# Attention order: the weight conversion's sum on VectorE with two more stops, q and k loaded one block sooner, x joined one block later

## The chip, the cores and the metric

The kernel runs on one core of one Trainium2 chip. The metric is the device time of one execution in microseconds (us). Before the change three runs took 835.17, 841.61 and 843.53 us; their median is 841.61 us.

Names used below: PE is TensorE, DVE is VectorE, ACT is ScalarE, POOL is GpSimd, SP is the engine whose one queue issues all DMAs of this kernel.

## What is computed

Clustered attention over 2 batches, 8 heads, 768 positions and head size 64, and then two gated feed-forward layers on its output. Cut to what matters:

```python
q_assign = np.argmax(np.einsum('bhsd,hcd->bhsc', q_n, c_n), axis=-1)   # nearest of 16 centroids
k_assign = np.argmax(np.einsum('bhsd,hcd->bhsc', k_n, c_n), axis=-1)
scores = np.where(q_assign[..., None] == k_assign[:, :, None, :], scale * q @ k.T, -1e9)
attn = softmax(scores); x = (attn @ v)                      # 1536 tokens x 512
x = ((x @ w1) * (x @ w2)) @ w3 @ w_out                      # d_ff = 1024
out = (sigmoid(x @ w_gate) * (x @ w_val)) @ w_out2          # d_ff = 1536
```

The weights arrive as 64-bit floats, two 32-bit words an element. The kernel turns each into a float32 pair (a rounded high part and the rest) and multiplies in three products (`mm3`).

## The kernel before

**Attention.** The 16 heads go as 8 pairs (`pr` 0 to 7). A pair has 6 blocks of 256 query rows (`at` 0 to 5); the loop at line 493 runs over all 48 blocks, `i`. For each block PE makes scores (128x768 tiles `s`), DVE their maxima (`nm`, line 348), ACT the exponentials (`e`, line 359), PE transposes these (`pt`, line 369), ACT copies the transposed tile to its high part (`ph`, line 387) and DVE makes the rest (`pl`, line 398); in three blocks of six one of the three pieces goes by way of a copy `pc` to POOL, which makes both parts. PE then multiplies by v (`av`, lines 410 and 411), and ACT copies the result to `xa` (line 419).

**Order by hand.** Inside `tc.manual_schedule` every engine, and SP's queue, executes in exactly the order in which the loop body is written. An instruction that waits holds up all that stands behind it on its engine. The work of other pairs is sprinkled over the six blocks:

- `load_qk(later)` asks for q and k (`raw`) of the pair after next, in block 1; `prep_split(later)` takes them on ACT in blocks 3 and 4 (`hi`, lines 236 and 56); `prep_scatter` copies the parts to their places with 6 DMAs per head.
- `take_x` also joins the two heads of the previous pair, in block 1: two DMAs into `xb` and a third, into `xa`, that has to wait for the first. `add_x` (POOL, block 3) adds the halves and fetches the row sums `r`; `norm_x` and `split_x` (POOL, block 5) finish that pair's 768 tokens of `x`.

**Conversion.** `f64_steps` turns one 128x512 half of a weight into its pair of parts: DMA, magnitude on ACT (line 108), clamp, shift, or, and, product (lines 115 to 124, all DVE here), sum (line 125, `f_engine`), high part on ACT (line 126), rest on POOL (line 127). It is a generator, and `convert(1)` runs it to its next `yield`: once in each of the blocks 2, 3, 4 and 5 of pairs 1 to 7, which makes 28 calls. Four halves are converted in this way: `w12_0_0`, `w12_0_1`, `w12_1_0`, `w12_1_1` (rows call their tiles `w_f`, `w_a` and `w`). The last piece of a half, from the product to the rest, runs in one go, and in the same call as the next half's DMA, so a half takes 6 calls. `convert(99)` behind the loop runs what is left.

**After attention** the scheduler, not the hand, sets the order. `g_unit(m, u)` multiplies x of 512 tokens by `wt[m]`; units (0,0) and (1,0) need tokens of batch 0 only, (0,1) needs the last pair. The other halves (`w_out` as `wo`, `w12`, `w3T`) are converted by the same generator, with a tile `w_t` in PSUM (lines 110 to 127), in 3 rotating buffers; the scheduler lets their first DMAs, ACT and POOL passes run already during attention, when a buffer is free. `w34_unit(0)` is the first to need `w3T`.

Of the kernel before, what the change touches and what calls it, by code (L numbers as in the profile page):

```python
# [8 lines left out]
F32 = mybir.dt.float32  # L9
# [6 lines left out]
B, H, S, D, C = 2, 8, 768, 64, 16  # L16
# [11 lines left out]
def tile_cluster_attention__then__moe__then__gated_moe(  # L28
# [15 lines left out]
    nc = tc.nc  # L44
# [16 lines left out]
    def move(dst, src):  # L61
        nc.sync.dma_start(dst.bitcast(F32), src.bitcast(F32))  # L62
# [36 lines left out]
    def f64_steps(src, hi, lo, name, f_engine, lo_engine):  # L99
# [22 lines left out]
        nc.vector.tensor_scalar(out=t, in0=high, scalar1=0xFF800000, scalar2=None, op0=ALU.bitwise_and)  # L122
        yield
        nc.vector.scalar_tensor_tensor(out=tf, in0=low, scalar=2.0 ** -52, in1=tf, op0=ALU.mult, op1=ALU.mult)
        f_engine.tensor_tensor(out=af, in0=high.bitcast(F32), in1=tf, op=ALU.add)
        nc.scalar.copy(hi, af)  # L126
        lo_engine.tensor_tensor(out=lo, in0=af, in1=hi, op=ALU.subtract)  # L127

    def pair_steps(src, m, what, f_engine):
        hl = ws.tile([128, 2, 2, NP, 128], F32R, tag="hl", name=f"{what}{m}")  # L130
        return hl, [
            f64_steps(src[m, w], hl[:, 0, w].rearrange("p k c -> p (k c)"), hl[:, 1, w].rearrange("p k c -> p (k c)"),
                      f"{what}{m}_{w}", f_engine, nc.gpsimd)
            for w in range(2)
        ]
# [277 lines left out]
    def take_x(i):  # L413
        if i not in avs:
            return
        pr, e, q0 = blocks[i]
        if q0 == 0:
            acc_x[pr, e] = core.tile([128, S], F32, tag=f"xa{e}", name=f"xa{pr}_{e}", bufs=2 - e)
        nc.scalar.copy(acc_x[pr, e][:, q0 : q0 + 256], avs.pop(i))  # L419
        if (e, q0) == (1, 512):  # L420

            xa, x1 = acc_x[pr, 0], acc_x.pop((pr, 1))
            xb = core.tile([128, S], F32, tag="xb", name=f"xb{pr}", bufs=1)
            move(xb[0:64], xa[64:128])
            move(xb[64:128], x1[0:64])
            move(xa[64:128], x1[64:128])
            acc_x[pr, "xb"] = xb

    def sums(pr):

# [53 lines left out]
                steps.pop(0)  # L484

    for m in range(2):
        hl, st = pair_steps(w12, m, "w12_", nc.gpsimd)
        wt.append(hl)
        steps += st
    with tc.manual_schedule(engines={mybir.EngineType.PE, mybir.EngineType.DVE, mybir.EngineType.Activation, mybir.EngineType.Pool, mybir.EngineType.SP}):  # L490
        for e in range(2):
            prep_v(0, e)
        for i in range(-2, NB + 2):
# [11 lines left out]
                prep_code(nxt)  # L505
            if nxt and at == 1:
                prep_scatter(nxt, 1)
            if later and at == 1:
                load_qk(later)
            split_lo(i - 1, 2)  # L510
            split_hi(i, 0)
            split_lo(i, 0)
# [60 lines left out]
            if 0 < pr < NPR and at == 3:  # L573
                convert(1)
        convert(99)
        for stage in (add_x, norm_x, split_x):
            stage(NPR - 1)
    att.close()

# [183 lines left out]
```

## Time and profile before

| what | value |
|---|---|
| three runs | 835.17, 841.61, 843.53 us |
| profiled execution, time | 838.32 us |
| its span, first to last instruction | 836.5 us |
| PE busy | 783.5 us, 94% |
| DVE, ACT, POOL busy | 581.8, 346.1, 348.1 us |
| pairs 1 to 5 of attention | 33.7 to 39.0 us each |
| pair 6 | 27.2 us |

A pair's stretch runs here from the reciprocal of the row sums of the pair before to its own. Busy time of an engine says how long instructions were in flight on it; a row of a timeline gives the start, the duration and in brackets how long the engine stood idle before it, and what ended that.

### The profile page before, as it was taken

How to read it: one execution, taken by the hardware profiler on the slowest of the kernel's cores; microseconds unless marked ns; L12 is line 12 of the kernel's file. 1: busy time of each engine (PE TensorE's matmuls, PEld its weight loads, DVE VectorE, ACT ScalarE, POOL GpSimd, SP SyncE). 2: the span in 40 equal slices, each digit the busy share in tenths (PEclk: the TensorE clock that was granted, in tenths of full speed). 3: DMA queues.
4: the chain of work that ended last, by engine and by line, in shares of the span. 5: the costliest groups of instructions: out<-in, count | busy, mean ns of one | idle time of the engine just before them, and what ended most of it. 6: DMA issues, size and time to landing. Idle time of an engine off the chain costs nothing.

```text
span 836.5 us, 11135 instructions
## 1 busy us (share of the span) xinstructions
PE 783.5 (94%) x4053; PEld 668.7 (80%) x4053; DVE 581.8 (70%) x848; ACT 346.1 (41%) x662; POOL 348.1 (42%) x358
## 2 busy tenths in 40 slices
PE   6897969879699889999999999999999999999998
PEld 5787958778598768887888888888888888888886
DVE  3797979879789757998899653177762577737322
ACT  1787767677578713443334221232232232013100
POOL 3354775557666634554445211034340343214200
PEclk8998999999889999999999999999999999999999
DMA  7558475484843142443444110012230122200012
GB/s 210 120 128 215 113 195 125 113 212 103 209 131 83 54 123 76 151 146 121 138 139 138 51 51 0 1 51 76 94 107 27 50 76 77 75 26 1 1 55 96
DMA packets 28887, 82.77 MB, mean 99 GB/s; under 512 B 4800, under 2 KB 4896, under 8 KB 28832
## 3 DMA queue, kind: packets, MB, share of 16 engines
q1 hardware_dynamic: 28832, 82.05, 34.2%
q8 instruction: 32, 0.52, 0.2%
q14 instruction: 23, 0.19, 0.1%
HBM read 52.49 MB, written 3.19 MB: 67 GB/s over the span
## 4 chain that ended last, share of the span: by engine, by line
PE 65%; DVE 9%; POOL 7%; DMA 7%; issue 6%; ACT 4%; SPq 2%; DVEq 0%; POOLq 0%; ACTq 0%
PE p L66 16%; PE p L67 16%; PE p L65 16%; PE pt L369 2%; PE av L410 2%; DMA w_f<-in_w_dram 2%; DVE nm L348 2%; DMA r<-r_dram 2%; PE av L411 2%; SPq L62 1%; DMA w_f<-in_w3T_dram 1%; PE w34p L67 1%; DVE pl L398 1%; PE w34p L66 1%; PE w34p L65 1%
## 5 line engine op out<-in xcount | busy, mean ns | idle before, releaser
L410 PE MATMUL av<-ph,vx 128*128 128x256 f32 x288 | 84.4, 320 | 35.3 <-ACT xa L419 34.7
L65 PE MATMUL p<-x,wgv 128*128 128x512 f32 x288 | 112.0, 389 | 0.0
L66 PE MATMUL p<-x,wgv 128*128 128x512 f32 x288 | 112.0, 389 | 0.0
L67 PE MATMUL p<-x,wgv 128*128 128x512 f32 x288 | 112.0, 389 | 0.0
L398 DVE TENSOR_TENSOR pl<-pt,ph 128x512 fp32r<-128x512 f32 x120 | 80.0, 682 | 32.0 <-ACT ph L387 30.6
L348 DVE TENSOR_REDUCE nm<-s 128x1 f32<-128x768 f32 x96 | 90.5, 944 | 11.0 <-PE s L341 10.5
L359 ACT ACTIVATE e<-s,nm 128x768 f32<-128x768 f32 x96 | 87.3, 909 | 20.0 <-DVE nm L348 18.9
L410 PEld LDWEIGHTS av<-ph,vx 128*128 128x128 f32 x288 | 57.0, 198 | 43.1 <-POOL w L127 16.1
L369 PE MATMUL pt<-ident,e 128*128 128x128 f32 x576 | 81.8, 280 | 0.6 <-DVE pl L398 0.6
L387 ACT CAST ph<-pt 128x512 fp32r<-128x512 f32 x120 | 69.1, 593 | 25.3 <-PE pt L369 23.8
L66 PE MATMUL p<-x,w 128*128 128x512 f32 x192 | 75.4, 393 | 1.4 <-POOL x L59 1.4
L411 PE MATMUL av<-pl,vx 128*128 128x256 f32 x288 | 76.1, 291 | 0.5 <-DVE pl L398 0.5
L65 PE MATMUL p<-x,w 128*128 128x512 f32 x192 | 75.5, 393 | 1.0 <-POOL x L54 1.0
L67 PE MATMUL p<-x,w 128*128 128x512 f32 x192 | 75.4, 393 | 0.0
L369 PEld LDWEIGHTS pt<-ident,e 128*128 128x128 f32 x576 | 70.0, 146 | 5.4 <-PE pt L369 0.9
L54 POOL TENSOR_SCALAR u<-ut 128x512 fp32r<-128x512 f32 x36 | 22.3, 620 | 112.1 <-DVE ut L689 112.1
L67 PEld LDWEIGHTS p<-x,wgv 128*128 128x128 f32 x288 | 54.1, 188 | 11.3
L65 PEld LDWEIGHTS p<-x,wgv 128*128 128x128 f32 x288 | 54.1, 188 | 11.2
L66 PEld LDWEIGHTS p<-x,wgv 128*128 128x128 f32 x288 | 54.1, 188 | 11.1
L127 POOL TENSOR_TENSOR wo<-wo_a,wo 128x512 fp32r<-128x512 f32 x20 | 26.3, 1313 | 81.0 <-ACT wo L126 81.0
L59 DVE TENSOR_TENSOR u<-ut,u 128x512 fp32r<-128x512 f32 x36 | 35.7, 991 | 34.1 <-POOL u L54 32.9
L411 PEld LDWEIGHTS av<-pl,vx 128*128 128x128 f32 x288 | 57.6, 200 | 0.7 <-DVE pl L398 0.7
(142 smaller groups left out, 1852.2 us busy)
## 6 DMA issues: line engine op xcount, KB each, us to landing
wgv_f<-in_w_gv_dram SPq DMA_DIRECT2D x24, 512.0 KB, 3.3
wo_f<-in_w_out_dram SPq DMA_DIRECT2D x20, 512.0 KB, 3.1
w_f<-in_w_dram SPq DMA_DIRECT2D x16, 512.0 KB, 3.2
w_f<-in_w3T_dram SPq DMA_DIRECT2D x16, 512.0 KB, 3.3
raw<-in_qkT_dram SPq DMA_DIRECT2D x16, 384.0 KB, 3.3
vraw<-in_v_dram SPq DMA_DIRECT2D x8, 384.0 KB, 4.1
QH<-hi SPq DMA_DIRECT2D x16, 192.0 KB, 5.7
KH<-hi SPq DMA_DIRECT2D x16, 192.0 KB, 3.6
```

Source lines behind the costliest of these rows:

```text
L59: lo_engine.tensor_tensor(out=lo, in0=x, in1=hi, op=ALU.subtract)
L65: nc.tensor.matmul(ps, whi, xhi, start=start, stop=False)
L66: nc.tensor.matmul(ps, whi, xlo, start=False, stop=False)
L67: nc.tensor.matmul(ps, wlo, xhi, start=False, stop=stop)
L127: lo_engine.tensor_tensor(out=lo, in0=af, in1=hi, op=ALU.subtract)
L348: nc.vector.tensor_reduce(out=nms[j], in_=sps[j][:, 0:S], axis=AX.X, op=ALU.max, negate=True)
L359: nc.scalar.activation(et, sps.pop(j)[:, 0:S], AF.Exp, bias=nms.pop(j), accum_out=acc_x[pr, "sum"][:, at : at + 1])
L369: nc.tensor.transpose(pt[:, kk, 128 * t : 128 * t + 128], exps[2 * i + t][:, k0 : k0 + 128], ident)
L387: nc.scalar.copy(ph, pt)
L398: nc.vector.tensor_tensor(out=pl, in0=src, in1=ph, op=ALU.subtract)
L410: nc.tensor.matmul(avs[i], w, ph[:, kk, :], start=kt == 0, stop=False)
L411: nc.tensor.matmul(avs[i], w, pl[:, kk, :], start=False, stop=kt == KT - 1)
```

## The change

Four edits. The sum of the four hand-scheduled halves goes from POOL to DVE. Two `yield`s are added, one before and one behind the sum, so a half takes 8 calls and not 6; with 28 calls three halves and the first four calls of the fourth stay inside the loop, and the rest of `w12_1_1` is run by `convert(99)`. `load_qk` moves from block 1 to block 0. The join of x becomes a function of its own, called in block 2.

```diff
         nc.vector.scalar_tensor_tensor(out=tf, in0=low, scalar=2.0 ** -52, in1=tf, op0=ALU.mult, op1=ALU.mult)
+        yield
         f_engine.tensor_tensor(out=af, in0=high.bitcast(F32), in1=tf, op=ALU.add)
+        yield
         nc.scalar.copy(hi, af)
         lo_engine.tensor_tensor(out=lo, in0=af, in1=hi, op=ALU.subtract)
...
         nc.scalar.copy(acc_x[pr, e][:, q0 : q0 + 256], avs.pop(i))
-        if (e, q0) == (1, 512):
-
-            xa, x1 = acc_x[pr, 0], acc_x.pop((pr, 1))
-            xb = core.tile([128, S], F32, tag="xb", name=f"xb{pr}", bufs=1)
-            move(xb[0:64], xa[64:128])
-            move(xb[64:128], x1[0:64])
-            move(xa[64:128], x1[64:128])
-            acc_x[pr, "xb"] = xb
+
+    def join_x(pr):
+
+        xa, x1 = acc_x[pr, 0], acc_x.pop((pr, 1))
+        xb = core.tile([128, S], F32, tag="xb", name=f"xb{pr}", bufs=1)
+        move(xb[0:64], xa[64:128])
+        move(xb[64:128], x1[0:64])
+        move(xa[64:128], x1[64:128])
+        acc_x[pr, "xb"] = xb
...
     for m in range(2):
-        hl, st = pair_steps(w12, m, "w12_", nc.gpsimd)
+        hl, st = pair_steps(w12, m, "w12_", nc.vector)
...
-            if later and at == 1:
+            if later and at == 0:
                 load_qk(later)
+            if at == 2 and 0 < pr and i < NB:
+                join_x(pr - 1)
...
         convert(99)
-        for stage in (add_x, norm_x, split_x):
+        for stage in (join_x, add_x, norm_x, split_x):
             stage(NPR - 1)
```

Three places show how the instructions move. In the changed program the lines behind the edits are 2 or 3 higher (125 is 126, 127 is 129, 439 is 442, 448 is 451).

**POOL, pair 2, blocks 4 and 5.** `ph` and `pl` are the parts of a transposed tile, `lo` the rest of k for pair 4, `w_0_0_a` the half under conversion, `xa` with `r` the norm of pair 1. Before:

```order
L54 TENSOR_SCALAR ph_0_1534<-pc_1536 128x512
L59 TENSOR_TENSOR pl_0_1535<-pc_1536,ph_0_1534 128x512
L59 TENSOR_TENSOR lo_1_1544<-raw_1_1327,hi_1_1543 128x768
L125 TENSOR_TENSOR w_0_0_a<-w_0_0_f_962,w_0_0_a 128x512
L127 TENSOR_TENSOR w_0_291<-w_0_0_a,w_0_291 128x512
L448 TENSOR_TENSOR xa_0_929<-xa_0_929,r_1472 128x768
```

After, the same place:

```order
L54 TENSOR_SCALAR ph_0_1534<-pc_1536 128x512
L59 TENSOR_TENSOR pl_0_1535<-pc_1536,ph_0_1534 128x512
L59 TENSOR_TENSOR lo_1_1544<-raw_1_1243,hi_1_1543 128x768
L451 TENSOR_TENSOR xa_0_925<-xa_0_925,r_1472 128x768
L54 TENSOR_SCALAR x<-xa_0_925 128x768
```

The sum is gone from POOL, and the rest (`w_0_291`) stands a pair's half later, in block 2 of pair 3; ACT's high part of the same half moved with it.

**SP's queue, from the row sums of pair 0 on, that is pair 1.** `QH`, `KH`, `QX` and `KX` are `prep_scatter`'s, `vraw` is v, `raw` q and k of pair 3. Before:

```order
L436 DMA r_dram<-rt_757 12x128
L216 DMA vraw_814<-in_v_dram 128x768
L62 DMA xb_847<-xa_0_485 64x768
L62 DMA xb_847<-xa_1_690 64x768
L62 DMA xa_0_485<-xa_1_690 64x768
L62 DMA QH_1_862<-hi_0_579 64x768
L62 DMA KH_1_863<-hi_1_644 64x768
L62 DMA QX_1_864<-hi_0_579 64x768
L62 DMA QX_1_864<-lo_0_580 64x768
L62 DMA KX_1_865<-lo_1_645 64x768
L62 DMA KX_1_865<-hi_1_644 64x768
L211 DMA raw_0_872<-in_qkT_dram 128x768
```

After:

```order
L439 DMA r_dram<-rt_757 12x128
L213 DMA raw_0_788<-in_qkT_dram 128x768
L213 DMA raw_1_790<-in_qkT_dram 128x768
L218 DMA vraw_818<-in_v_dram 128x768
L62 DMA QH_1_862<-hi_0_579 64x768
L62 DMA KH_1_863<-hi_1_644 64x768
L62 DMA QX_1_864<-hi_0_579 64x768
L62 DMA QX_1_864<-lo_0_580 64x768
L62 DMA KX_1_865<-lo_1_645 64x768
L62 DMA KX_1_865<-hi_1_644 64x768
L62 DMA xb_937<-xa_0_485 64x768
L62 DMA xb_937<-xa_1_690 64x768
```

The two loads of q and k moved past v, the join and the six scatters, to the head; the join moved behind the scatters.

**POOL, the end of attention.** `xa_0_3597` (before) and `xa_0_3583` (after) is the last pair's x, `xa_0_3200` and `xa_0_3186` that of pair 6, `wo` the first half of `w_out`. Before:

```order
L448 TENSOR_TENSOR xa_0_3200<-xa_0_3200,r_3680 128x768
L54 TENSOR_SCALAR x<-xa_0_3200 128x768
L59 TENSOR_TENSOR x<-xa_0_3200,x 128x768
L439 TENSOR_TENSOR xa_0_3597<-xa_0_3597,xb_3843 128x768
L448 TENSOR_TENSOR xa_0_3597<-xa_0_3597,r_3848 128x768
L54 TENSOR_SCALAR x<-xa_0_3597 128x768
L59 TENSOR_TENSOR x<-xa_0_3597,x 128x768
L127 TENSOR_TENSOR wo<-wo_a,wo 128x512
```

After:

```order
L451 TENSOR_TENSOR xa_0_3186<-xa_0_3186,r_3671 128x768
L54 TENSOR_SCALAR x<-xa_0_3186 128x768
L110 TENSOR_SCALAR wo_a<-wo_a 128x512
L59 TENSOR_TENSOR x<-xa_0_3186,x 128x768
L110 TENSOR_SCALAR w_2_0_a<-w_2_0_a 128x512
L129 TENSOR_TENSOR w_1_292<-w_1_1_a,w_1_292 128x512
L442 TENSOR_TENSOR xa_0_3583<-xa_0_3583,xb_3843 128x768
L110 TENSOR_SCALAR w_2_1_a<-w_2_1_a 128x512
L451 TENSOR_TENSOR xa_0_3583<-xa_0_3583,r_3848 128x768
L54 TENSOR_SCALAR x<-xa_0_3583 128x768
L59 TENSOR_TENSOR x<-xa_0_3583,x 128x768
```

The rest of `w12_1_1` (`w_1_292`) now stands ahead of the last pair's addition, and the clamp of `w_2_1` between that addition and the norm; the clamps of `wo` and `w_2_0` came here from pair 6.

## Rows read from the trace of the kernel before

**Rows 1.** The page: the span, and part 1, busy time of each engine.

```profile
span 836.5 us, 11135 instructions
...
PE 783.5 (94%) x4053; PEld 668.7 (80%) x4053; DVE 581.8 (70%) x848; ACT 346.1 (41%) x662; POOL 348.1 (42%) x358
```

**Rows 2.** Busy time by stretch, the pairs 1, 2, 4, 5 and 6 of attention; columns: stretch and its length, PE, PE's weight loads, DVE, ACT and POOL busy (instructions), granted clock as a share of full speed, DMA share, GB/s.

```profile
58.40:92.50 34.10, 29.36 (x204) 27.11 (x203) 28.34 (x39) 24.46 (x51) 20.45 (x18) 0.90 0.66 161
92.50:129.20 36.70, 29.03 (x203) 26.66 (x202) 29.58 (x41) 24.98 (x53) 23.56 (x20) 0.95 0.60 150
...
162.90:198.40 35.50, 29.22 (x204) 26.81 (x204) 30.07 (x40) 24.87 (x52) 23.35 (x20) 0.95 0.61 155
198.40:237.40 39.00, 31.49 (x202) 29.05 (x201) 29.68 (x40) 25.05 (x53) 23.53 (x20) 0.87 0.58 141
237.40:264.60 27.20, 26.73 (x198) 24.54 (x198) 26.16 (x38) 22.64 (x49) 19.84 (x20) 1.00 0.56 148
```

**Rows 3.** Who waited for whom, from 25 to 293 us; us in total, times, longest.

```profile
PE av L410 <- ACT xa L419: 34.7, 18, 5.1
...
ACT w L126 <- POOL w_a L125: 15.7, 4, 4.5
```

**Rows 4.** Timeline of PE: the eight starts of `av` behind an idle time that the prediction counts.

```profile
81.42 0.58 PE L410 MATMUL av<-ph,vx 128*128 128x256 f32 x1 [4.74 <-ACT xa L419]
...
113.30 0.38 PE L410 MATMUL av<-ph,vx 128*128 128x256 f32 x1 [1.18 <-ACT xa L419]
122.77 0.42 PE L410 MATMUL av<-ph,vx 128*128 128x256 f32 x1 [5.06 <-ACT xa L419]
...
150.12 0.38 PE L410 MATMUL av<-ph,vx 128*128 128x256 f32 x1 [1.59 <-ACT xa L419]
...
181.06 0.55 PE L410 MATMUL av<-ph,vx 128*128 128x256 f32 x1 [4.18 <-ACT xa L419]
...
220.67 0.39 PE L410 MATMUL av<-ph,vx 128*128 128x256 f32 x1 [2.65 <-ACT xa L419]
230.15 0.55 PE L410 MATMUL av<-ph,vx 128*128 128x256 f32 x1 [3.47 <-ACT xa L419]
...
281.03 0.36 PE L410 MATMUL av<-ph,vx 128*128 128x256 f32 x1 [2.52 <-ACT xa L419]
```

**Rows 5.** Timeline of ACT: `hi` of q in pairs 1, 2, 3 and 5, one magnitude (line 108) and one high part of the conversion (line 126).

```profile
77.03 0.84 ACT L236 ACTIVATE hi<-raw 128x768 fp32r<-128x768 f32 x1 [2.56 <-DMA raw<-in_qkT_dram]
80.44 0.66 ACT L108 ACTIVATE w_a<-w_f 128x512 f32<-128x512 f32 x1 [1.21 <-DMA w_f<-in_w_dram]
...
110.77 0.85 ACT L236 ACTIVATE hi<-raw 128x768 fp32r<-128x768 f32 x1 [1.10 <-issue]
...
120.37 0.62 ACT L126 CAST w<-w_a 128x512 fp32r<-128x512 f32 x1 [4.53 <-POOL w_a L125]
...
147.59 0.85 ACT L236 ACTIVATE hi<-raw 128x768 fp32r<-128x768 f32 x1 [1.55 <-issue]
...
218.15 0.84 ACT L236 ACTIVATE hi<-raw 128x768 fp32r<-128x768 f32 x1 [2.62 <-DMA QH<-ohT]
```

**Rows 6.** Timeline of POOL in pair 2, in front of ACT's high part at 120.37.

```profile
116.84 2.25 POOL L59 TENSOR_TENSOR lo<-raw,hi 128x768 fp32r<-128x768 f32 x1
119.05 1.28 POOL L125 TENSOR_TENSOR w_a<-w_f,w_a 128x512 f32<-128x512 f32 x1
121.06 1.27 POOL L127 TENSOR_TENSOR w<-w_a,w 128x512 fp32r<-128x512 f32 x1 [0.73 <-ACT w L126]
```

**Rows 7.** Timeline of SP's queue in pair 2 (a duration is that of the issue).

```profile
92.61 0.33 SPq L436 DMA_DIRECT2D r_dram<-rt  x1
96.11 0.36 SPq L216 DMA_DIRECT2D vraw<-in_v_dram  x1
...
106.66 1.20 SPq L211 DMA_DIRECT2D raw<-in_qkT_dram  x2
```

**Rows 8.** The lines of the conversion, the forms that run during attention; ns shortest, median, longest, first and last start.

```profile
L115 DVE TENSOR_SCALAR w_a<-w_a x4: 415/1414/1516, 83.8 to 248.8; 128x512 f32<-128x512 f32 x4
...
L118 DVE TENSOR_SCALAR w_a<-w_a x4: 414/536/779, 89.3 to 255.4; 128x512 uint32<-128x512 uint32 x4
...
L120 DVE SCALAR_TENSOR_TENSOR w_f<-w_f,w_a x4: 1090/1600/1780, 103.8 to 257.3; 128x512 uint32<-128x512 uint32 x4
...
L122 DVE TENSOR_SCALAR w_a<-w_f x4: 416/416/771, 112.7 to 262.3; 128x512 uint32<-128x512 uint32 x4
...
L124 DVE SCALAR_TENSOR_TENSOR w_a<-w_f,w_a x4: 921/1680/1777, 115.7 to 275.3; 128x512 f32<-128x512 uint32 x4
```

**Rows 9.** Timelines of PE and POOL at the end of attention: PE's wait for the last `pl`, POOL's last addition of x, PE's two waits for the last pair's x.

```profile
293.15 0.38 PE L411 MATMUL av<-pl,vx 128*128 128x256 f32 x1 [0.45 <-DVE pl L398]
...
298.30 1.85 POOL L439 TENSOR_TENSOR xa<-xa,xb 128x768 f32<-128x768 f32 x1 [5.43 <-DMA xa<-xa]
...
307.73 0.49 PE L65 MATMUL p<-x,w 128*128 128x512 f32 x1 [1.02 <-POOL x L54]
309.62 0.50 PE L66 MATMUL p<-x,w 128*128 128x512 f32 x1 [1.39 <-POOL x L59]
```

**Rows 10.** Who waited for whom, PE alone, from 300 us to the end: one of three lines.

```profile
PE w34p L67 <- POOL w L127: 0.6, 1, 0.6
```

**Rows 11.** Busy time by stretch, 300 to 320 us (columns as in rows 2).

```profile
300.00:320.00 20.00, 17.59 (x69) 13.84 (x68) 8.39 (x13) 3.37 (x7) 7.77 (x7) 0.91 0.37 123
```

## The prediction, made before the changed kernel ran

> **What bounds the kernel now.** Read the page first: PE is busy 94% of an 836.5 us span [rows 1], so what can be won is the time in which PE stands still. The list of waits puts nearly all of that in one place: in attention PE's `av` waits 34.7 us, 18 times, put down to ACT's copy `xa` [rows 3]. A copy of 0.4 us is not slow; it stands behind something on ACT. The stretches by pair then show what a pair costs with and without these waits: pair 6 takes 27.2 us with PE busy for 26.73, while pairs 1, 2, 4 and 5 take 34.1 to 39.0 with about the same PE work [rows 2]. They also show the second engine in line: DVE is busy for 26.16 of the 27.2 us of pair 6, and for about 28 to 30 us in the others [rows 2]. So a pair can't shrink below what DVE needs, some 28 to 31 us.
>
> The timelines say what holds ACT up. Two causes cover eight of PE's waits. (a) The conversion's high part (line 126) waits for the sum on POOL: 15.7 us on ACT in four times [rows 3]. The sum takes only 1.28 us, but it stands in POOL's queue behind the 2.25 us of `lo`, and ACT stops for 4.53 us [rows 5, 6], with the exponentials and `xa` behind it. PE's four waits from it are 5.06, 4.18, 3.47 and 2.52, together 15.2 us [rows 4]. (b) `hi` of q waits for the load: 2.56, 1.10, 1.55 and 2.62 us on ACT, and a magnitude 1.21 more behind the first [rows 5]. PE's waits from these are 4.74, 1.18, 1.59 and 2.65, together 10.2 us [rows 4]. The list names other releasers for two of the four ("issue"); the load is the last one issued ahead of them, so I count them with it.
>
> **The change, part by part.**
>
> *The two stops and the sum on DVE.* ACT's high part now runs in a later call than the sum; between them lie blocks of other work, so ACT finds the sum done. Wait (a) goes: -15.2 us. In its place DVE gets three sums in attention (the fourth comes behind the loop). No row of before has a DVE sum with both operands and result in SBUF. The nearest is the product of line 124, same shape, one operand strided: 0.921 to 1.777 us, median 1.68 [rows 8]; below nothing is excluded, since the engine has to read 512 elements. I take 1.68. The calls also move between pairs: even pairs now carry or, and, product and sum, odd pairs only clamp and shift. By the medians of rows 8 a full even pair is 1.60 + 0.42 + 1.68 + 1.68 = 5.4 us. Pair 2 had the first three, so +1.7. Pair 4 had product, clamp and shift, 3.6, so +1.7. Pair 6 had clamp, shift, or and and, 4.0, so +1.4. Pairs 3 and 5 get lighter by about 2 us each, which I count at nothing since PE bounds them. DVE is the engine next in line in even pairs, so I let all 4.8 us come back to PE. The bounds: nothing, if DVE fills the gaps in which it waits now, and 7 us, with every instruction at its longest.
>
> The Trainium skill has a rule that speaks against this edit: SBUF — State Buffer, "Who interferes with whom", says that a VectorE instruction with two SBUF inputs and a GpSimd instruction that reads SBUF exclude each other for the whole instruction. The trace agrees in kind: the product takes 0.921 us at its shortest and 1.777 at its longest [rows 8]. By the rule the three sums would cost their longest, 5.3 us, by the row's median 5.0; what it would do to POOL is a rival below.
>
> *q and k sooner.* What matters is SP's queue, not the block: the load stands at 106.66 us behind v, the join and six scatters, though the queue passed `r_dram` at 92.61 [rows 7]. The new place is right behind `r_dram`, ahead of v, which waits until 96.11 for its buffer. The loads' own buffers are free by then (`lo` of k was read in block 4). So they go out some 13 us sooner, against waits of 1.1 to 2.6 us on ACT [rows 5]. Wait (b) goes: -10.2 us. If the load went out only a block sooner (about 5 us) it would still do. The magnitude's DMA behind it also gets out sooner, since the two loads are no longer in front.
>
> *x later.* The scatters move ahead of the join by three DMAs, the join behind six; SP sends it about 5 us later, and POOL's addition is two blocks away, about 9 us at 27.2 / 6 = 4.5 us a block [rows 2]. Cost: none, by a thin margin. What hides it is POOL's own slack, busy 23.56 of 36.7 us [rows 2]; without that cover it would cost 1 or 2 us in each of seven pairs.
>
> *The handover.* `w12_1_1` is now half done when attention ends. The last `pl` ends at about 293.1 (PE starts on it at 293.15 [rows 9]). Behind it DVE has or, and, one shift of `wo`, the product, an or of `wo`, the sum. With the shortest of rows 8 that is 1.09 + 0.42 + 0.41 + 0.92 + 1.09 + 0.92 = 4.9 us, with the medians 1.60 + 0.42 + 0.54 + 1.68 + 1.60 + 1.68 = 7.5. Then 0.62 on ACT and 1.27 on POOL [rows 5, 6]: done at 299.9 to 302.5. POOL's last addition stands behind that and started at 298.30 [rows 9]: it is late by 1.6 to 4.2 us. I take 2.8, about the middle, since POOL, whose instructions stretch DVE's, is nearly idle here. PE, which waited 1.02 and 1.39 us for the x that comes of it [rows 9], waits that much longer: +2.8. `wt[1]` itself is in time, since PE asks for its second half only after the 36 products of unit (0,0) and the first half of (1,0), at 17.59 / 69 = 0.25 us each [rows 11] near 302.5. Conversions later on are just in time (PE waits 0.6 us once for the rest of a `w3T` half [rows 10]). I let them slip with PE and cost that at nothing, because DVE is busy for only 8.39 us of the 20 behind 300 [rows 11]; without that cover it is up to 4 us.
>
> **Sum.** -15.2 - 10.2 + 4.8 + 2.8 = -17.8 us. From the profiled execution, 836.5 + 1.8 around the span = 838.3, that gives 820.5. The median of the three runs is 841.6, 3.3 above the profiled execution, the lowest 835.2, below it. I add half of the 3.3 and forecast 822 us.
>
> **The rivals.**
>
> 1. *More than the sum.* After its long waits PE runs slowly for a while: pair 5 has a granted clock of 0.87 and 31.49 us of PE busy, pair 6 1.00 and 26.73 [rows 2]. Without the waits that comes back too, and pairs 3 and 5 lose DVE work. Pairs 1 to 5 at pair 6's 27.2 and 1.4 for the centroid products that it lacks would be 28.6, pairs 2 and 4 with 1.7 more. Against lengths of 34.1, 36.7, 33.7, 35.5 and 39.0 that is 32.6 off; with pair 6 1.4 longer, pair 7 2.5 shorter and the handover 2.8, -31 at the utmost. Half way from the sum: 815.
>
> 2. *DVE and POOL take over.* If each of three sums collides with a POOL instruction in front of it or behind, DVE and POOL both lose up to 1.7 us a time, and the exponentials, which wait for DVE's maxima, stop PE in ACT's place; half of the 25.4 us stays. -12.7 + 4.8 + 2.8 = -5.1, with the same additions 835. For it: DVE is 96% busy in pair 6 [rows 2]. Against: while ACT stops DVE idles too, so the room for the sums is there. By that rule of the skill's page this is where the time would end; the trace agrees as to the long products, and can't show the sums.
>
> 3. *The load doesn't go sooner*, because SP is held up ahead of it. Then only (a) goes: -15.2 + 4.8 + 2.8 = -7.6, 832. Against: the queue stands at `r_dram` 14 us before the load [rows 7].
>
> 4. *Slower: the handover grows.* The late half moves the last addition, the norm behind the clamp of `w_2_1`, and every conversion behind them; since these are just in time, PE would wait again at `w34_unit(0)`. It decides when the lateness passes 20.6 us, of which my bounds (4.2 and 4) explain 8.2. At 29 it would be 848.
>
> **Chances.** The sum as it stands, 815 to 829: 0.66. Rival 1: 0.10. Rival 2: 0.14. Rival 3: 0.06. Rival 4: 0.04. The range 812 to 832 leaves out rival 4, most of rival 2 and the end of rival 1, together under 2 in 10. A measurement of this kernel tells 1% from no change, that is below 833.2 and above 850. Faster holds the first case, rival 1, rival 3 and a third of rival 2: 0.86; the same 0.11; slower 0.03.
>
> **What would show it.** In the profile after: no wait of ACT's conversion copy for a sum; SP's load right behind `r_dram` and no wait of `hi`; `av`'s waits for `xa` near 35 - 25 + 5 = 14 us, in pairs 2, 4 and 6 and behind DVE's maxima; pairs 3 and 5 under 31 us; sums on DVE of 0.9 to 1.8 us; PE's wait for the last x near 5 us. The forecast is wrong if the waits come back under another name (maxima, `pl`), if POOL waits for the join in block 3, or if PE's wait behind 300 us passes 10 us.

## The result and the profile after

The changed kernel takes 817.86 us in the median of 4 runs (814.42 to 818.6), the kernel before 840.31 in the median of 4 (the three above and one of 839.01): a ratio of 0.973 with a 95% interval of 0.967 to 0.979. The forecast was 822 in a range of 812 to 832, so the time lies inside it. The profiled execution went from a span of 836.5 us to 816.5.

The page of the kernel after, the rows that answer to [rows 1]:

```profile
span 816.5 us, 11135 instructions
...
PE 776.9 (95%) x4053; PEld 662.3 (81%) x4053; DVE 584.3 (72%) x852; ACT 346.1 (42%) x662; POOL 344.2 (42%) x354
```

Where did the 20 us go? The best way in is to cut both executions at the same two events, the reciprocals that end pair 0 and pair 7. Busy time by stretch of the kernel before (stretch and length, PE, PE's weight loads, DVE, ACT, POOL, granted clock, DMA share, GB/s):

```profile
0.00:57.55 57.55, 46.48 (x306) 41.80 (x307) 39.18 (x61) 32.75 (x63) 22.37 (x35) 0.94 0.67 165
57.55:291.61 234.06, 199.31 (x1387) 183.37 (x1386) 194.46 (x262) 167.54 (x353) 147.00 (x130) 0.94 0.55 139
291.61:836.50 544.89, 537.69 (x2364) 443.57 (x2363) 348.19 (x526) 145.76 (x248) 178.71 (x194) 1.00 0.22 75
```

The same three stretches after:

```profile
0.00:59.96 59.96, 49.52 (x306) 44.88 (x307) 39.27 (x62) 32.86 (x63) 22.53 (x35) 0.89 0.64 158
59.96:271.22 211.26, 191.09 (x1387) 175.10 (x1386) 194.16 (x261) 166.23 (x351) 139.28 (x122) 0.99 0.58 152
271.22:816.50 545.28, 536.27 (x2364) 442.29 (x2363) 350.87 (x530) 147.04 (x250) 182.37 (x198) 1.00 0.23 76
```

Read the middle rows. Pairs 1 to 7 became 22.8 us shorter. PE's idle time there (length less busy) fell from 34.75 to 20.17, by 14.6; its busy time fell by 8.2 for the same 1387 matmuls, at a granted clock of 0.99 where it was 0.94. Pair 0 became 2.4 longer, at a lower clock; the rest of the program, the handover included, 0.4 longer. -22.8 + 2.4 + 0.4 = -20.0, the difference of the spans.

By pair, the pairs 1 to 6 after (columns as before; these answer to [rows 2]). One row there is cut at other events than the rest: its pair 6 begins at the end of one reciprocal and ends at the start of the next, 1.1 us short. Cut as below, pair 6 of the kernel before takes 28.28 us and not 27.20:

```profile
236.34:264.62 28.28, 27.80 (x205) 25.53 (x204) 27.11 (x39) 23.09 (x50) 19.86 (x20) 1.00 0.54 143
```

After:

```profile
59.96:91.28 31.32, 27.57 (x203) 25.37 (x202) 28.36 (x39) 24.20 (x50) 20.40 (x18) 1.00 0.68 177
91.28:122.47 31.19, 27.81 (x205) 25.52 (x204) 30.25 (x40) 23.80 (x51) 21.39 (x19) 1.00 0.63 159
122.47:153.26 30.79, 27.60 (x201) 25.12 (x200) 28.23 (x38) 24.67 (x53) 21.67 (x20) 1.00 0.68 178
153.26:184.44 31.18, 27.82 (x205) 25.52 (x204) 30.24 (x40) 23.81 (x51) 21.37 (x19) 1.00 0.63 159
184.44:216.88 32.44, 28.64 (x200) 26.33 (x199) 28.52 (x39) 25.31 (x56) 21.66 (x20) 0.95 0.66 169
216.88:246.04 29.16, 27.78 (x205) 25.56 (x204) 28.27 (x39) 22.09 (x46) 19.09 (x18) 1.00 0.41 103
```

Pairs 1 to 5 are now alike, 30.8 to 32.4 us. In the even ones DVE is busy for all but one us of the length: there it leaves no room, as the extra sum below shows. In the odd ones it is busy for 28.2 to 28.5, and PE still stands still for over 3 us. The waits of the kernel after, from 25 to 275 us (us in total, times, longest), say at what:

```profile
ACT e L361 <- DVE nm L350: 27.6, 39, 2.0
PE av L412 <- ACT xa L421: 20.5, 20, 2.0
```

No wait of ACT for the sum is left in this stretch, and none of `hi` for the load. PE's starts of `av` behind an idle time, against [rows 4]:

```profile
81.07 0.39 PE L412 MATMUL av<-ph,vx 128*128 128x256 f32 x1 [2.01 <-ACT xa L421]
...
87.24 0.35 PE L412 MATMUL av<-ph,vx 128*128 128x256 f32 x1 [1.74 <-ACT xa L421]
...
107.39 0.36 PE L412 MATMUL av<-ph,vx 128*128 128x256 f32 x1 [1.35 <-ACT xa L421]
...
118.16 0.36 PE L412 MATMUL av<-ph,vx 128*128 128x256 f32 x1 [2.01 <-ACT xa L421]
...
149.22 0.35 PE L412 MATMUL av<-ph,vx 128*128 128x256 f32 x1 [1.74 <-ACT xa L421]
```

None is longer than 2.01, and eleven are of 1.00 us or more. Eight of the eleven stand behind DVE. For the one at 149.22, in pair 3, DVE's timeline and ACT's:

```profile
144.13 1.35 DVE L240 SCALAR_TENSOR_TENSOR lo<-raw,hi 128x768 fp32r<-128x768 f32 x1
145.41 1.51 DVE L115 TENSOR_SCALAR w_a<-w_a 128x512 f32<-128x512 f32 x1
146.84 0.94 DVE L350 TENSOR_REDUCE nm<-s 128x1 f32<-128x768 f32 x1
...
147.82 0.90 ACT L361 ACTIVATE e<-s,nm 128x768 f32<-128x768 f32 x1 [1.73 <-DVE nm L350]
```

The maximum `nm` stands behind the rest of q and the conversion's clamp, together 2.8 us; the exponential waits 1.73 for it, `xa` stands behind the exponential, and PE waits 1.74. Pairs 1 and 5 have the same wait. In even pairs the clamp's place is taken by the product (waits of 2.01 and 1.99), and another maximum stands behind `or` (three waits of 1.35).

The other three, 2.01, 1.00 and 1.57 us, one in each odd pair, stand behind the conversion's magnitude on ACT. In pairs 1 and 5 that waits for its DMA, 1.16 and 0.64 us; in pair 3 it has no wait, and ACT is busy all the while with `hi`, an exponential and the magnitude. The one in pair 1, ahead of the wait at 81.07:

```profile
80.10 0.66 ACT L108 ACTIVATE w_a<-w_f 128x512 f32<-128x512 f32 x1 [1.16 <-DMA w_f<-in_w_dram]
80.66 0.36 ACT L421 COPY xa<-av 128x256 f32<-128x256 f32 x1
```

SP's queue in pair 2, against [rows 7]: the load of q and k now goes out right behind `r_dram`, 14 us sooner, and v no later than before.

```profile
92.25 0.33 SPq L439 DMA_DIRECT2D r_dram<-rt  x1
92.63 0.82 SPq L213 DMA_DIRECT2D raw<-in_qkT_dram  x2
95.76 0.33 SPq L218 DMA_DIRECT2D vraw<-in_v_dram  x1
```

### The profile page after: what moved, and what is told of

The parts are those of the page before. It is cut to its first block, busy times and chain, and to the rows that moved or that the text cites. A ratio compares the mean times of both kernels' runs of the same rounds, so it can differ in the third digit from the quotient of the medians.

```text
span 816.5 us, 11135 instructions
## 1 busy us (share of the span) xinstructions
PE 776.9 (95%) x4053; PEld 662.3 (81%) x4053; DVE 584.3 (72%) x852; ACT 346.1 (42%) x662; POOL 344.2 (42%) x354
## 3 DMA queue, kind: packets, MB, share of 16 engines
q1 hardware_dynamic: 28832, 82.05, 34.7%
## 4 chain that ended last, share of the span: by engine, by line
PE 65%; DVE 12%; DMA 6%; POOL 5%; issue 5%; ACT 4%; SPq 2%; DVEq 0%; ACTq 0%; POOLq 0%
PE p L66 17%; PE p L67 17%; PE p L65 17%; PE pt L371 3%; DVE nm L350 2%; DVE pl L400 2%; PE av L412 2%; DMA w_f<-in_w3T_dram 2%; PE sims L270 1%; PE av L413 1%; PE w34p L67 1%; PE w34p L66 1%; PE w34p L65 1%; DMA xb<-xa 1%; SPq L62 1%
## 5 line engine op out<-in xcount | busy, mean ns | idle before, releaser
L412 PE MATMUL av<-ph,vx 128*128 128x256 f32 x288 | 80.9, 310 | 20.8 <-ACT xa L421 20.5
L361 ACT ACTIVATE e<-s,nm 128x768 f32<-128x768 f32 x96 | 87.3, 909 | 28.6 <-DVE nm L350 27.6
L400 DVE TENSOR_TENSOR pl<-pt,ph 128x512 fp32r<-128x512 f32 x120 | 79.8, 680 | 14.2 <-ACT ph L389 11.9
L412 PEld LDWEIGHTS av<-ph,vx 128*128 128x128 f32 x288 | 54.5, 189 | 28.7 <-POOL lo L59 10.3
L413 PE MATMUL av<-pl,vx 128*128 128x256 f32 x288 | 72.8, 282 | 0.5 <-DVE pl L400 0.5
L54 POOL TENSOR_SCALAR u<-ut 128x512 fp32r<-128x512 f32 x36 | 22.3, 619 | 112.1 <-DVE ut L694 112.1
L59 DVE TENSOR_TENSOR u<-ut,u 128x512 fp32r<-128x512 f32 x36 | 35.7, 991 | 34.1 <-POOL u L54 32.9
L694 DVE TENSOR_TENSOR ut<-p,ut 128x512 f32<-128x512 f32 x36 | 24.7, 686 | 44.4 <-PE p L67 44.3
```

The lines of the kernel that those rows point to most:

```text
L59: lo_engine.tensor_tensor(out=lo, in0=x, in1=hi, op=ALU.subtract)
L361: nc.scalar.activation(et, sps.pop(j)[:, 0:S], AF.Exp, bias=nms.pop(j), accum_out=acc_x[pr, "sum"][:, at : at + 1])
L400: nc.vector.tensor_tensor(out=pl, in0=src, in1=ph, op=ALU.subtract)
L412: nc.tensor.matmul(avs[i], w, ph[:, kk, :], start=kt == 0, stop=False)
L413: nc.tensor.matmul(avs[i], w, pl[:, kk, :], start=False, stop=kt == KT - 1)
```

## The experiments

Each kernel was timed on one chip with the kernel before in the same batch (medians of before: 838.7, 837.99 and 838.04 us in three batches). All ratios are to before.

### Which edit brings the time: each alone, and both without the join

*The two stops and the sum on DVE, alone* (from the kernel before):

```diff
+        yield
         f_engine.tensor_tensor(out=af, in0=high.bitcast(F32), in1=tf, op=ALU.add)
+        yield
...
-        hl, st = pair_steps(w12, m, "w12_", nc.gpsimd)
+        hl, st = pair_steps(w12, m, "w12_", nc.vector)
```

> The kernel before with the two stops and the sum on VectorE alone; load and join stay where they were. If the prediction's sum is right, ACT's conversion copy no longer waits for a sum (15.7 us gone), PE's four waits behind it (15.2 us) go, up to 4.8 us come back through VectorE and about 2 at the handover: span 826 to 830 us, and ACT still waits for the load of q in four pairs (about 8 us). If the two causes overlap, so that removing one exposes the other, the span stays above 832 us and the waits for the load grow by as much.

Measured: 831.76 us, ratio 0.994 (0.989 to 1.000): by the interval no gain is shown for this edit alone. The profiled span, 829.5 us, is in the first branch, but what happened is the second: ACT's waits for the sum are gone and waits for DMAs have grown (below).

*The load of q and k in block 0, alone* (from the kernel before):

```diff
-            if later and at == 1:
+            if later and at == 0:
                 load_qk(later)
```

> The kernel before with q and k asked for one block sooner alone. If the prediction's sum is right, ACT's waits for the load go and with them PE's 10.2 us: span about 826 us, ACT's four waits for the sum on POOL (15.7 us) stay. If the join, which in this kernel still stands ahead of the six scatters, was what held the load up, the load goes out sooner all the same but the scatters behind it run late, and the gain is under 5 us: span above 831 us.

Measured: 832.86 us, ratio 0.994 (0.991 to 0.997): 5.8 us by the medians, where 10.2 were expected. The profiled span, 833.7 us, is in the second branch. The waits for the load in pairs 2, 3 and 5 are gone. But in pair 1 the magnitude now waits 2.39 us for its DMA and PE still 3.24, where it was 4.74; and in pair 5, where PE no longer waits for the load, its wait for the sum on POOL grew from 3.47 to 5.04, while ACT's stayed (4.54 and 4.52).

*Both, with the join of x back in block 1* (from the kernel after):

```diff
             take_x(i - 2)
+            if at == 1 and 0 < pr and i < NB:
+                join_x(pr - 1)
...
-            if at == 2 and 0 < pr and i < NB:
-                join_x(pr - 1)
```

> The changed kernel with the join of x put back into block 1, ahead of the scatters. The prediction costs the later join at nothing: span within 1.5 us of the changed kernel's 816.5. If moving the join was part of the gain (it keeps SP from stopping for its first DMA ahead of the scatters), the span is 3 us or more above it; if the later join costs something at POOL's addition, where the profile of the changed kernel shows waits of 0.4 to 1.0 us, it is 1 to 3 us below.

Measured: 819.9 us, ratio 0.979 (0.975 to 0.982).

The two edits are not two sums that add. By the medians each alone is worth 0.6%, both together 2.1%. Pairs 1 to 7 of each profiled execution, worked out from the stretches by pair as above:

| kernel | length, us | PE busy | PE idle |
|---|---|---|---|
| before | 234.06 | 199.31 | 34.75 |
| stops and sum on DVE | 227.27 | 195.50 | 31.77 |
| load sooner | 228.77 | 199.27 | 29.50 |
| both, join in block 1 | 215.91 | 195.13 | 20.78 |
| after | 211.26 | 191.09 | 20.17 |

Idle time falls by 3.0 and 5.2 alone and by 14.0 together. The trace of the stops alone shows why. ACT waits no more for the sum, but PE's longest waits are still there, 5.73, 6.35 and 5.03 us, in pairs 1, 3 and 5. ACT in that kernel, in the pairs 1 and 3:

```profile
76.36 0.84 ACT L238 ACTIVATE hi<-raw 128x768 fp32r<-128x768 f32 x1 [2.33 <-DMA raw<-in_qkT_dram]
...
81.00 0.66 ACT L108 ACTIVATE w_a<-w_f 128x512 f32<-128x512 f32 x1 [2.42 <-DMA w_f<-in_w_dram]
...
151.64 0.66 ACT L108 ACTIVATE w_a<-w_f 128x512 f32<-128x512 f32 x1 [3.74 <-DMA w_f<-in_w_dram]
```

and SP's queue ahead of the first of these:

```profile
71.88 1.47 SPq L213 DMA_DIRECT2D raw<-in_qkT_dram  x2
73.40 0.47 SPq L103 DMA_DIRECT2D w_f<-in_w_dram  x1
```

With 8 calls a half, and 8 calls in two pairs, each half's DMA falls in the same place of an odd pair, right behind the late load of q and k. The magnitude then waits for it on ACT in all three. With 6 calls a half, as before, only the first waited for longer than half a microsecond [rows 5]. So the stops bring the halves into step with the late load, and the wait taken from the sum comes back under the name of a DMA. The sooner load takes that away in pairs 3 and 5: with both edits and the join in block 1 the magnitude waits there for nothing and for 0.57 us. In pair 1 it still waits 2.54, and that takes the later join.

*Is it the DMA's place?* The stops alone again, with the DMAs of the first three halves issued in pair 0 already:

```diff
+            if 3 <= i < 6:
+                next(steps[i - 3])
             scores(2 * i + 4)
```

> The kernel before with the stops and the sum on VectorE (as the run with these alone), and with the DMAs of the first three halves sent in pair 0; load and join stay where they were. In the run with the stops alone ACT waited 11.0 us for the halves' DMAs, which stand right behind the late loads of q and k. If that is what ate the gain of the stops, these waits go and the span is 817 to 823 us against 829.5. If the late load itself is what holds ACT, its waits (8 us) stay or grow and the span is 826 or more.

Measured: 832.31 us, ratio 0.991 (0.988 to 0.994). The first branch missed; the second is where it ended, for `hi` still waits 8.2 us in five pairs, 1.09 to 2.23 each (8.6 with the stops alone). The waits for these three DMAs are gone and pairs 1 to 7 take 221.77 us, 5.5 less than with the stops alone. But the calls move with them, by one in the first half and by three in the fourth, whose DMA is now late (ACT waits 3.62 us); and behind attention the program takes 549.79 us against 545.13. So the DMAs' place, together with the calls that move, has 5.5 of the 11.4 us that lie between the stops alone and both edits. The rest I put down to the waits of `hi` and of the fourth half, by their rows on ACT alone; no run takes them apart. Why the later stage lost 4.7 us is not shown; one magnitude waits 5.56 us for its DMA there, at 290.37.

*The join.* With it in block 1, one wait of the kind above comes back, in pair 1: in the kernel with both edits and the join in block 1,

```profile
80.60 0.66 ACT L108 ACTIVATE w_a<-w_f 128x512 f32<-128x512 f32 x1 [2.54 <-DMA w_f<-in_w_dram]
...
81.57 0.58 PE L412 MATMUL av<-ph,vx 128*128 128x256 f32 x1 [3.42 <-ACT xa L421]
```

and pair 1 takes 34.67 us against 31.32. In the six variants below that keep the join in block 2 and the DMAs where they were, pair 1 takes 30.80 to 32.10. The times of the two kernels (819.9 and 817.86) have intervals that overlap, so the gain of the later join is shown in the trace and not in the time.

### Which half of the first edit is needed

*The sum back on POOL, stops kept* (from the kernel after):

```diff
-        hl, st = pair_steps(w12, m, "w12_", nc.vector)
+        hl, st = pair_steps(w12, m, "w12_", nc.gpsimd)
```

> The changed kernel with the sum back on POOL, both stops kept. If the stops are what takes ACT off POOL's queue and VectorE is the engine next in line, ACT's copy still waits for nothing and the three sums of about 1.04 us leave VectorE: span 813 to 816 us. If the engine of the sum was what mattered, ACT's copy waits for POOL again, 2 us or more a time, and the span is 820 us or more.

Measured: 818.83 us, ratio 0.977 (0.974 to 0.980).

*Only the stop ahead of the sum* (from the kernel after; the sum stays on DVE):

```diff
         f_engine.tensor_tensor(out=af, in0=high.bitcast(F32), in1=tf, op=ALU.add)
-        yield
         nc.scalar.copy(hi, af)
```

> The changed kernel without the stop behind the sum, so that ACT's copy is issued right behind VectorE's sum, in one call; a half takes 7 calls and all four halves fit into the 28. If it is the stop that frees ACT, ACT waits for VectorE's sum four times, each as long as VectorE is behind (1 to 3 us), PE with it: span 820 to 824 us in spite of a shorter handover. If moving the sum off POOL's queue is enough, ACT's four waits are under 0.5 us and the span is 813 to 817.

Measured: 821.08 us, ratio 0.978 (0.973 to 0.982).

Neither differs from the kernel after by more than the intervals allow, and neither expectation is met cleanly: the first span (817.0) lies between its branches, and in the second run the profiled span (816.5) fits the second branch, the median of the times doesn't. With the stop behind the sum ACT has no wait for it even where POOL makes it; with the sum on DVE and no stop there, ACT's high part waits 0.92, 1.45 and 0.39 us, where it was up to 4.53 [rows 5]. The stop and the other engine are two remedies for one wait of 15.7 us in all: inside attention the stop behind the sum takes all of it away, the other engine without that stop all but 2.8. With the sum on POOL, pairs 1 to 7 even take 1.5 us less (209.75). The end of attention gives it back (550.2 us behind pair 7 against 545.3), as PE's wait for the last x in that kernel shows against 1.42 after:

```profile
287.29 1.22 PE L65 MATMUL p<-x,w 128*128 128x512 f32 x2 [4.68 <-POOL x L54]
```

### What DVE's time costs PE

*One more sum on DVE ahead of each of the four* (from the kernel after; its result isn't used):

```diff
+        if not cvp:
+            nc.vector.tensor_tensor(out=low.bitcast(F32), in0=high.bitcast(F32), in1=tf, op=ALU.add)
         f_engine.tensor_tensor(out=af, in0=high.bitcast(F32), in1=tf, op=ALU.add)
```

> The changed kernel with one more VectorE sum of the same operands (its result goes to words that nobody reads) right in front of each of the four sums. It prices a VectorE instruction in blocks 5 of pairs 2, 4 and 6, which the prediction let come back to PE in full. If so, the span grows by three times 1.04 and 0.7 at the handover, to 819.5 to 821; if VectorE has room there, it stays within 1 us of 816.5.

Measured: 823.43 us, ratio 0.981 (0.977 to 0.984). DVE's work in pair 2 grows by 2.19 us (to 32.44) and the pair by 2.23:

```profile
57.81:89.00 31.19, 29.20 (x203) 26.89 (x202) 28.47 (x38) 24.31 (x50) 20.40 (x18) 0.95 0.69 178
89.00:122.42 33.42, 29.82 (x206) 27.22 (x205) 32.44 (x42) 23.84 (x51) 21.38 (x19) 0.95 0.59 149
122.42:152.87 30.45, 27.20 (x197) 24.95 (x198) 28.24 (x39) 24.69 (x53) 21.68 (x19) 1.00 0.68 180
```

Pairs 4 and 6 grow by 2.26 and 1.97; pairs 1, 3 and 5 don't grow. So in an even pair a microsecond more on DVE is a microsecond of the pair. The span, 821.4 us, is a little over the first branch, since the second sum took 2.2 us in each of these pairs and not 1.04. The other way it is worth less: with the sum on POOL the even pairs are only 0.32 to 0.36 us shorter than after.

*The clamp on POOL* (from the kernel after), which takes 1.51 us from DVE in odd pairs:

```diff
-            nc.vector.tensor_scalar(out=af, in0=af, scalar1=F64_MAX, scalar2=F64_MIN, op0=ALU.min, op1=ALU.max)
+            nc.gpsimd.tensor_scalar(out=af, in0=af, scalar1=F64_MAX, scalar2=F64_MIN, op0=ALU.min, op1=ALU.max)
```

> The changed kernel with the clamp of the four halves on POOL in place of VectorE, where it takes 1.51 us in block 4 of pairs 1, 3 and 5, next to the rest of q (1.2 us), and ACT's exponentials then wait 1.7 us for a maximum. If that pile-up on VectorE is what is left of PE's waits in the odd pairs, their waits of 1.74, 1.74 and 1.75 us go and the span is 811 to 814. If something else sets the odd pairs (ACT or PE itself), the span stays at 816 or more.

Measured: 814.7 us, ratio 0.970 (0.967 to 0.973), the lowest median of all, though the interval overlaps that of the kernel after. The waits of 1.74, 1.74 and 1.75 fall to 0.30 or 0.31, so the clamp is what made them; PE's `av` waits fall from 20.5 us to 16.0, and pairs 1 to 7 take 209.08 us, 2.2 less than after. Pairs 1, 3 and 5 are 0.52, 0.46 and 1.98 shorter. The last of these isn't the clamp's alone: pair 5 after has a granted clock of 0.95, here 1.00, and at 1.00 it took 30.73 and 30.99 us with the clamp on DVE (in the run with the extra sum and in the next one), 30.46 here. So the odd pairs are held up by DVE too, but by about half a microsecond each; what holds the rest of PE's idle time there, 1.7 to 2.5 us a pair, no run takes apart. The clamp on POOL takes 0.62 us each time.

### The end of attention, and the remedies together

*All four halves finished inside the loop*, by four more calls in the last pair (from the kernel after):

```diff
+            if pr == NPR - 1 and at in (0, 1, 3):
+                convert(1)
...
+            if pr == NPR - 1 and at == 4:
+                convert(1)
```

> The changed kernel with four more calls in the last pair (blocks 0, 1, 3 and 4), so that only the copy and the rest of the fourth half stand behind the loop. The prediction's handover term was 2.8 us for the last addition of x, which stands behind that half on POOL; the profile of the changed kernel shows that addition 0.5 to 1 us late at most. If the handover costs the 2.8, the span falls to about 814; if only what the profile shows, to 815 to 816.5, and PE's 1.4 us wait for a high part of w3T goes or stays by how the other halves follow.

Measured: 815.71 us, ratio 0.971 (0.966 to 0.975). PE's first wait for the last x falls from 1.42 to 0.88 us and the last pair takes 25.97 us against 25.18: nothing is won that the intervals can show. The span, 815.6 us, is that of the second branch.

*Clamp and sum on POOL, all four halves inside* (the three edits above together):

> The changed kernel with the clamp and the sum of the four halves on POOL, both stops kept, and the four more calls in the last pair, so that the fourth half is done inside the loop. VectorE loses 1.51 us in each odd and 1.04 us in each even pair against the changed kernel. If VectorE's busy time sets these pairs and the handover is kept short by the extra calls, the span is 809 to 812 us. If POOL becomes the one that is waited for (its clamp and sum stand behind the rest of k), ACT or VectorE waits for it and the span stays above 815.

Measured: 817.83 us, ratio 0.976 (0.972 to 0.980), no gain over the clamp alone. The span, 816.6 us, is in the second branch, but not for its reason: ACT's one wait for the sum on POOL is 0.56 us. Attention ends sooner, pairs 1 to 7 in about 210 us, but POOL's last addition hardly does: in that kernel it starts at 277.75, behind the join's DMA (after: 278.82), and PE, which is there sooner, waits longer for the x that comes of it.

```profile
277.75 1.85 POOL L442 TENSOR_TENSOR xa<-xa,xb 128x768 f32<-128x768 f32 x1 [2.26 <-DMA xa<-xa]
284.03 1.80 POOL L451 TENSOR_TENSOR xa<-xa,r 128x768 f32<-128x768 f32 x1 [4.43 <-DMA r<-r_dram]
...
286.80 0.79 PE L65 MATMUL p<-x,w 128*128 128x512 f32 x1 [4.23 <-POOL x L54]
```

*The same, with the first three DMAs in pair 0:*

> The kernel of the run with clamp and sum on POOL and all four halves inside the loop, with the DMAs of the first three halves sent in pair 0, which also moves every later step of the conversion by three calls. ACT's waits for these DMAs (about 2 us in two places) go. If the steps land no worse on VectorE than before, the span is 1 to 3 us under that run; if they pile up on the heavy blocks 4 and 5, it is 1 to 4 us over it.

Measured: 821.63 us, ratio 0.980 (0.977 to 0.984), worse than that run, inside the second branch. In pairs 3 and 5 `or` and `and` now stand behind the rest of q, together 3.9 and 3.6 us between two maxima, and the exponentials wait 3.08 and 2.81 us, PE 3.89 and 3.64; in pair 6 the fourth half's magnitude waits 3.84 for its DMA and PE 3.66.

## Why the prediction was right, step by step

The forecast of 822 held, in part by luck: the sum behind it reached its value by errors that cancel. In the terms of the profiled execution it said -17.8 and -20.0 was measured.

**The two waits: right for both together, wrong as two separate gains.** The causes that the two steps named for the eight waits of [rows 4] are gone, at the places that the prediction gave for it (ACT's high part without a wait, the load right behind `r_dram`). The prediction says that the list names another releaser for two of `hi`'s four waits; in [rows 5] it is three, the last a DMA of the scatters. That none of the four is left bears its reading out. One piece stayed: in pair 1 the magnitude still waits 1.16 us for its DMA, before 1.21, since that goes out only 1.0 us sooner against the pair's start (15.3 us behind it, before 16.3). But the working priced (a) at 15.2 and (b) at 10.2 as if each stood by itself. The three kernels show idle time falling by 3.0 and 5.2 for one edit and by 14.0 for both. What the sentence "the magnitude's DMA behind it also gets out sooner" mentioned in passing is the link: the stops put the halves' DMAs behind the load, and only the sooner load, in pair 1 with the later join, makes the stops pay. Rival 3, which gave the first edit alone 832 in the median, has its number from the run of the first edit alone: 831.76, by another road.

**What comes back: 11, not 4.8.** This is the term that was mis-sized most. The eight waits are 25.4 us, yet PE's `av` waits fell only by 14.2, from 34.7 to 20.5. Two things came back.

The first is DVE. Waits behind a late maximum weren't new: before there were five of them, 7.5 us, among the waits that [rows 4] leaves out. Three of these:

```profile
107.75 0.35 PE L410 MATMUL av<-ph,vx 128*128 128x256 f32 x1 [1.35 <-ACT xa L419]
...
156.55 0.36 PE L410 MATMUL av<-ph,vx 128*128 128x256 f32 x1 [2.01 <-ACT xa L419]
...
193.45 0.36 PE L410 MATMUL av<-ph,vx 128*128 128x256 f32 x1 [1.74 <-ACT xa L419]
```

After there are eight, 13.3 us. In the even pairs they rose by 5.0, near the predicted 4.8, but behind `or` and the product and not behind the sum, which was cheaper than taken: 1.03, 1.04 and 0.68 us in attention against 1.68 each. In pairs 3 and 5, which get lighter and were counted at nothing, they fell by 0.9 (4.4 to 3.5). In pair 1 the clamp's wait of 1.74 is new, though the clamp stood there before as well: the long wait had covered it. In the run of the stops alone, where each odd pair keeps a wait of over 5 us, none of them has the clamp's.

The second is ACT, and the prediction had no term for it. It moves the calls between pairs on DVE only; on ACT they bring each half's magnitude into an odd pair, right behind `hi`, where the waits for the load had been. The step that failed is "Wait (b) goes: -10.2 us". In place of three of its four waits (4.74, 1.59 and 2.65) there are now 2.01, 1.00 and 1.57 us behind the magnitude; pairs 2 and 4, with `hi` and no magnitude at that place, have none.

By idle time (-14.6) the result lies about half way between the sum (-25.4 + 4.8 = -20.6) and rival 2 (-12.7 + 4.8 = -7.9).

**PE's clock: 8.2 us that the sum didn't have.** Rival 1 named the cause, that PE runs slower after its long waits, but as a case apart. The run of the stops alone agrees: its pairs 1, 3 and 5, with a wait of over 5 us each, have a granted clock of 0.90 or 0.91, the even ones 1.00. After, without waits of over 2.01 us, the clock of pairs 1 to 7 went from 0.94 to 0.99 and PE's busy time from 199.31 to 191.09. In the bookkeeping this about makes up for the waits that came back. It is not what the clock alone was worth: in the run with all halves inside, pair 1 has a clock of 0.95 and 29.19 us of PE busy in 31.07 us, after 1.00 and 27.57 in 31.32, so there a slower PE cost idle time and not length.

**The handover: 0.4, not 2.8.** From PE's last wait for a `pl` to its second for x it was 16.47 us [rows 9] and is 16.88 (272.76 to 289.64). DVE's six instructions took 0.68 to 1.06 each, those with two inputs all below the shortest of [rows 8] for their lines, and the sum ended at 276.84. After, POOL and PE:

```profile
277.58 1.30 POOL L129 TENSOR_TENSOR w<-w_a,w 128x512 fp32r<-128x512 f32 x1 [3.41 <-ACT w L128]
278.82 1.86 POOL L442 TENSOR_TENSOR xa<-xa,xb 128x768 f32<-128x768 f32 x1
...
284.94 1.84 POOL L451 TENSOR_TENSOR xa<-xa,r 128x768 f32<-128x768 f32 x1 [3.38 <-DMA r<-r_dram]
...
287.75 0.50 PE L65 MATMUL p<-x,w 128*128 128x512 f32 x1 [1.42 <-POOL x L54]
289.64 0.50 PE L66 MATMUL p<-x,w 128*128 128x512 f32 x1 [1.39 <-POOL x L59]
```

The addition stands behind the rest of `w12_1_1` and started when that ended, 6.06 us behind PE's last wait for a `pl`. Before it was 5.15 (298.30 less 293.15), and 5.36 with all four halves inside, where it waits for the join's DMA. It is late by 0.9; even the lower end of the working, 1.6, was too much. PE's two waits for x are 2.8 us together, before 2.4, where the prediction looked for 5. The slip of later conversions, costed at nothing, is one new wait of 1.4 us for a half of `w3T`; the whole stretch behind attention is 0.4 longer.

**The join: nothing was charged, and in the trace it gained.** In pair 1 PE waits 2.01 us behind the magnitude, and 3.42 with the join in block 1.

**Not foreseen: pair 0.** It took 2.4 us more, at a lower clock, and the clock of that stretch differs as much between executions of the same order (below). Without it the profiled execution, 818.6 us, would have come out near 816.

**The signs that the prediction named.** The conversion's copy and `hi` without waits, the load behind `r_dram` and two sums of 0.9 to 1.8 us are there. `av`'s waits are 20.5 us and not 14, and nearly half of them lie in odd pairs; pair 3 is under 31 us, pair 5 (32.44) is not. One sign of being wrong showed in part, waits under another name: ACT's waits for maxima rose to 27.6 us, in the same list of before (25 to 293 us) they are 18.9. Pair 6's 27.2 us, in rival 1 and in the 4.5 us a block, should be 28.3; the sum doesn't use it.

Term by term, from the sum to what was measured: -17.8, + 6.0 of idle time that stayed, - 8.2 of clock, - 2.4 of handover, + 2.4 in pair 0, is -20.0.

## What to carry to other kernels

Two waits on one in-order engine that are fed from one in-order DMA queue are not priced by adding their idle times: undo each alone on paper, and see which other step then falls in behind the late transfer. When the longest waits go, ask what stands right behind each of them and was covered by it, on the released engine as well as on the next one; here the magnitude on ACT and pair 1's clamp on DVE came to light so. When calls move, follow them on every engine. And PE's idle time and its granted clock are two terms of one sum: cut the stretch at the same events in both traces and split length into busy and idle before saying which step was right, and don't take the two for independent.

## What the runs showed of the hardware

**DVE and POOL wait for each other, instruction by instruction.** With the extra sum, DVE and POOL in pair 2:

```profile
117.48 1.03 DVE L127 TENSOR_TENSOR w_f<-w_f,w_a 128x512 f32<-128x512 f32 x1
118.54 2.19 DVE L128 TENSOR_TENSOR w_a<-w_f,w_a 128x512 f32<-128x512 f32 x1
...
117.13 0.83 POOL L54 TENSOR_SCALAR x<-xa 128x768 fp32r<-128x768 f32 x1
118.05 2.13 POOL L59 TENSOR_TENSOR x<-xa,x 128x768 fp32r<-128x768 f32 x1
```

The same sum takes 0.68 us where POOL does nothing, 1.03 here and 2.19 one instruction later. The first ends 0.55 us behind POOL's L54 (117.96), the second 0.55 behind POOL's L59 (120.18); POOL's L59 in turn, 1.81 us at its shortest in this kernel, is 0.3 longer; it had begun 0.46 us before the first sum ended. The Trainium skill says this of such a pair (SBUF — State Buffer, "Who interferes with whom": a VectorE instruction with two SBUF inputs and a GpSimd instruction that reads SBUF exclude each other for the whole instruction), and these rows agree. So an instruction of this kind costs its own half microsecond and what is left of POOL's, and its place decides between 0.68 and 2.2 us more than its engine does. In the kernel after, the three sums met a short instruction of POOL's, or came first.

**The clock early in pair 0 differs between executions of the same order.** From 28 to 34 us the granted clock was 0.54 in the profiled execution after, near the lower of its two levels (1.2 and 2.4 GHz), and 1.00 in the one before. First after, then the kernel with the clamp on POOL, whose pair 0 has the same order as after:

```profile
28.00:34.00 6.00, 5.34 (x23) 4.77 (x21) 4.49 (x5) 4.46 (x9) 1.83 (x1) 0.54 0.46 122
```

```profile
28.00:34.00 6.00, 5.38 (x31) 4.31 (x32) 5.04 (x7) 5.27 (x12) 1.83 (x1) 1.00 0.54 136
```

In the first PE got 23 matmuls done in these 6 us, in the second 31, and pair 0 ended at 59.96 and 57.56 us. Of the thirteen profiled executions, four had 0.52 to 0.54 there and ended pair 0 at 59.8 to 60.0, one had 0.72 and ended it at 59.0, and eight had 1.00 and ended it at 57.1 to 57.9; the late and the sooner load are in both groups. What makes the clock fall there is not shown. That is 2.4 us between two executions that no edit explains, more than several of the differences above; it is why pairs 1 to 7 are compared here, and not spans.
